# Seven block products per pair of token tiles in a second mixture layer

## The chip, the core and the metric

One core of a Trainium2 chip runs attention and two mixture layers as one kernel. Its engines are TensorE (PE), VectorE (DVE), ScalarE (ACT), GpSimd (POOL) and SyncE (SP), which issues the DMAs. The metric is the device time of one execution in microseconds; less is better.

## The reference, cut to what matters

```python
def _moe2_ref(x, w_in, w_out, g_ln):          # x: 2304 x 512, w_in: 512 x 1024, w_out: 1024 x 512
    h = x @ w_in
    h_max = np.max(h, axis=-1, keepdims=True)
    e = np.exp(h - h_max)
    sm = e / (np.sum(e, axis=-1, keepdims=True) + 1e-09)
    solu = h * sm
    mu = np.mean(solu, axis=-1, keepdims=True)
    var = np.mean((solu - mu) ** 2, axis=-1, keepdims=True)
    ln = (solu - mu) / np.sqrt(var + 1e-06) * g_ln
    return ln @ w_out
```

Ahead of it stand causal attention with a decay (32 heads, 576 positions, 64 wide) and a first mixture layer of 2304 x 512 tokens with 2048 hidden units, whose result is this layer's x. The weights come in 64-bit floats; the kernel turns each chunk into 32-bit values itself.

## The kernel before, in words

Every product is made of three: each operand is split into a high part and a low part (a rounded 32-bit format of TensorE, and what it leaves), and high x high, high x low and low x high are summed in PSUM.

The order of the work isn't written out by hand. All work is handed to a planner (`add` of class Plan) as operations with an engine, a cost in ns (`dve(n)`, `act_p(n)`, `mm(n)`), the keys that they read and write, and a priority; `run` goes through a modelled time, lets each engine take the ready operation of lowest priority value (TensorE) or lowest ready time plus priority (the others), and writes the instructions out in that order. On the chip each engine's queue is in that order, and semaphores hold an instruction until its operands are there. DMAs are all issued from SP's queue, in order.

Attention comes first, with the first mixture layer's early jobs between (256 tokens each, three of eight groups of weights). Then `extend` closes attention's memory, and wide jobs of 512 tokens (`job_wide`) finish the first layer: first the other tokens with the first three groups, then all tokens with the other five. The last job has 256 tokens. While these run, the second layer's weights are loaded (`load_w`): a raw chunk of 512 KB is converted by ScalarE and VectorE (lines 805 to 812), and split into a high and a low part (lines 392 to 403 or 824 to 826). All eight weight tiles (128 x 1024, high and low) stay in SBUF: slots w0 to w5 and two late ones.

The second layer runs over 18 tiles of 128 tokens (`tile2`). For each pair of tiles the x of 256 tokens (512 deep, 4 chunks of 128) is loaded, cast to its high part (line 392) and subtracted to its low part (line 402). A tile's first product is four groups of six products of 128x512 (line 1125) into a PSUM tile of two banks, `ph`, of which there are two. Then VectorE takes the maximum of 1024 (line 1130), ScalarE the exponential (1132), VectorE the reciprocal and h times softmax (1135) and the centring (1138), ScalarE the squares (1139), GpSimd the inverse root. TensorE transposes the centred tile in two groups of four (line 1156); ScalarE makes the high part (1159), VectorE the low part (1160); 24 products (lines 1168 to 1170) give the output, which ScalarE scales (1174) and a DMA writes.

Tile 0's first product goes to the first layer's banks (`x2`), with priorities among the last job's products. `second` opens the second layer's pools when everything ahead has ended except DMAs (key m2); `third` gives the first layer's banks to transposes and outputs when tile 0's softmax is done with them (key m3). In the planner the first products of a later tile have priority 5000 + i, its transposes 5100 + i, its outputs 5200 + i.

Of the kernel before, what the change touches and what calls it, by code (L numbers as in the profile page):

```python
# [18 lines left out]
CH = 256  # L19
# [11 lines left out]
HM = 3  # L31
# [227 lines left out]
def kernel(  # L259
# [39 lines left out]
    xc_d = dram.tile([KD, 128, NT], F32, name="xc_d")  # L299

# [487 lines left out]
    def load_w(t, srcs, key, raws, sc=None, b=BW, after=()):  # L788

        for g, src in enumerate(srcs):  # L790
            hi, lo = (lambda x=x, g=g: x[:, 512 * g:512 * g + 512] for x in t)
            rn = slot(raws, 2)
            rt = rawsets[raws][rn]
            kr = (raws, rn)
            scv = None if sc is None else sc[:, g:g + 1]
            jr = slot("wr", 2)
            r = wr[jr]
            kw = ("wr", jr)
            add("SP", 650, lambda rt=rt, src=src: nc.sync.dma_start(
                out=rt()[:, :, 0:2 if wide else 1].rearrange("p (c n) e -> p c (n e)", c=src.shape[1]),  # L800
                in_=src.bitcast(U32)), (), [kr], b, bytes=524288, after=after)
            if wide:


                add("ACT", act_s(512), lambda rt=rt, r=r: nc.scalar.activation(
                    out=f32(r), in_=f32(rt())[:, :, 1], func=AF.Abs, scale=2.0 ** -112), [kr], [kw], b)
                add("DVE", dve2(512), lambda r=r: nc.vector.tensor_scalar(
                    out=r, in0=r, scalar1=3, scalar2=None, op0=ALU.logical_shift_left), (), [kw], b, lk=True)
                add("DVE", dve(512), lambda rt=rt, r=r: nc.vector.scalar_tensor_tensor(
                    out=r, in0=rt()[:, :, 0], scalar=29, in1=r, op0=ALU.logical_shift_right, op1=ALU.bitwise_or),  # L810
                    [kr], [kw], b, lk=True)
                add("DVE", dve(512), lambda rt=rt, r=r: nc.vector.scalar_tensor_tensor(
                    out=r, in0=rt()[:, :, 1], scalar=0x80000000, in1=r, op0=ALU.bitwise_and, op1=ALU.bitwise_or),
                    [kr], [kw], b, lk=True)
                rv = lambda r=r: f32(r)
                kv = kw
            else:
                rv = lambda rt=rt: f32(rt())[:, :, 0]
                kv = kr
            if sc is None:  # L820
                copy(hi, rv, 512, [kv], [key + (g, 0)], b)
                tt(lo, rv, lambda hi=hi: f32(hi()), 512, ALU.subtract, [kv, key + (g, 0)], [key + (g, 1)], b)
            else:
                add("ACT", act_s(512), lambda rv=rv, hi=hi, scv=scv: nc.scalar.activation(
                    out=hi(), in_=rv(), func=AF.Copy, scale=scv), [kv, "gl"], [key + (g, 0)], b)
                add("DVE", dve(512), lambda rv=rv, hi=hi, lo=lo, scv=scv: nc.vector.scalar_tensor_tensor(
                    out=lo(), in0=rv(), scalar=scv, in1=f32(hi()), op0=ALU.mult, op1=ALU.subtract),
                    [kv, "gl", key + (g, 0)], [key + (g, 1)], b, lk=True)
# [8 lines left out]
    def load_fp(fp, ta, tb, ka, kb, raws, b=BW, after=()):  # L837
        c = slice(fp * 256, fp * 256 + 256)
        a = w_in[:, c].rearrange("(k p) n -> p k n", p=128)
        load_w(ta, (a[:, 0:2], a[:, 2:4]), ka, raws, None, b, after)  # L840
        a = w_out[c, :].rearrange("(k p) n -> p k n", p=128)
        load_w(tb, (a[:, 0:1], a[:, 1:2]), kb, raws, None, b, after)
        weights[fp] = (ta, tb, ka, kb)
# [245 lines left out]
    NTILE = NT // 128  # L1089

    def tile2(i, part=None):

        c, o = divmod(i, 2)
        o *= 128
        jc, jh, jd, js = c % 2, i % 2, i % 3, i % 4
        kx = [H(("xx", 2)), H(("xx", 3))] if c == 0 else [[("x2h", jc)], [("x2l", jc)]]
        x_hi = (lambda: xhis[0]) if c == 0 else (lambda: late["xh"][jc])
        x_lo = (lambda: xlos[0]) if c == 0 else (lambda: late["xl"][jc])
        if i == 0:
            h = lambda: x2ps[0].rearrange("p k n -> p (k n)")  # L1100
            kh, ke, kd, ks, ext, ext2 = ("x2", 0, 0), ("wraw", 0), ("wraw", 1), "sm0", [], []
            e, d = (lambda t=t: f32(t).rearrange("p n e -> p (n e)") for t in wraw)
            sm = lambda: sm0
        else:
            h, e, d, sm = (lambda a=a, b=b: late[a][b] for a, b in (("ph", jh), ("e2", jh), ("d2", jd), ("sm", js)))
            kh, ke, kd, ks, ext, ext2 = ("ph", jh), ("e2", jh), ("d2", jd), ("sm", js), ["m2"], ["m2"]
        if o == 0 and c:
            t, kt = (lambda: xraw, H(("xx", 0))) if c == 1 else (lambda: late["xr"][jc], [("xr", jc)])
            add("SP", 650, lambda: nc.sync.dma_start(
                out=t(), in_=x2_d[:, :, c * CH:(c + 1) * CH].rearrange("k p t -> p k t")),  # L1110
                [("x2d", c, k) for k in range(KD)] + (ext if c > 1 else []),
                kt, 0, bytes=524288)
            copy(x_hi, t, 1024, kt + ext, kx[0], B2)
            tt(x_lo, t, lambda: f32(x_hi()), 1024, ALU.subtract, kt + kx[0], kx[1], B2)
        sp = lambda a: sm()[:, a:a + 1]
        V, A = nc.vector, nc.scalar
        if part == 1:
            return tile2_out(i, jd, d, sp, kd, ks)
        for kc in range(KD):
            def h_mm(kc=kc):  # L1120
                wh, wl = w2[kc]
                a, b = x_hi()[:, kc, o:o + 128], x_lo()[:, kc, o:o + 128]
                for st_, mv in ((a, wh), (a, wl), (b, wh)):
                    for n in range(0, DFF2, 512):
                        nc.tensor.matmul(h()[:, n:n + 512], st_, mv[:, n:n + 512],  # L1125
                                         start=kc == 0 and mv is wh and st_ is a, stop=kc == KD - 1 and st_ is b)

            add("PE", 6 * mm(512), h_mm, kx[0] + kx[1] + wkeys((f"w{kc}",)) + ext, [kh] + ([("x2", 0, 1)] if i == 0 else []),
                5000 + i if i else 1000 + 100 * (len(jobs) - 1) + (4 * HM if kc < KD - 1 else 99))
        add("DVE", dve(1024), lambda: V.tensor_reduce(out=sp(0), in_=h(), axis=AX.X, op=ALU.max), [kh], [ks], B3)  # L1130
        add("DVE", 70, lambda: V.tensor_scalar_mul(out=sp(1), in0=sp(0), scalar1=-1.0), (), [ks], B3)
# [11 lines left out]
        if part is None:  # L1143
            tile2_out(i, jd, d, sp, kd, ks)
# [132 lines left out]
    for i in range(8):  # L1277
        t = wslot[i] if i < 2 * FP1 else (Lazy(), Lazy())
        if i >= 2 * FP1:
            late["w2b", i - 2 * FP1] = t  # L1280
# [12 lines left out]
    for i in range(1, NTILE):  # L1293
        tile2(i)
# [44 lines left out]
```

## Time and profile before

| | us |
|---|---|
| Median of 3 runs | 833.92 (833.08 to 834.3) |
| The profiled execution | 835.25 |
| Its span, first to last instruction | 833.5 |
| TensorE busy, of the span | 808.5 (97%) |
| VectorE / ScalarE busy | 501.0 / 505.7 |
| Share of TensorE in the chain that ended last | 80% |

The span is what the trace shows; 1.75 us of the profiled execution lie around it. A product's record ends when its pipe has drained (0.39 us for 512 columns), while the next one starts earlier, so records of one engine overlap, and the distance of starts is the price of a product.

### The profile page before, as it was taken

To read this page: it belongs to the slowest core of one execution; us is meant where nothing else is said; L and a number is where in the kernel's file an instruction comes from. 1 tells how busy PE (TensorE), PEld (TensorE's weight loads), DVE (VectorE), ACT (ScalarE), POOL (GpSimd) and SP (SyncE) were. 2 spreads that over 40 slices of the span, in tenths; PEclk is the share of its full clock that TensorE was granted. 3 is DMA by queue.
4 is the path that set the end of the run, shared out by engine and by line. 5 is a ranking of instruction groups with operands and counts; after the bars stand their busy time and mean duration, and the time that the engine had idled before them with its cause. 6 is when DMAs were issued, how large, how long until landed. Compare 5 with 4: busy or idle time off the path is not lost.

```text
span 833.5 us, 12764 instructions
## 1 busy us (share of the span) xinstructions
PE 808.5 (97%) x4687; PEld 688.0 (83%) x4687; DVE 501.0 (60%) x1030; ACT 505.7 (61%) x1021; POOL 105.6 (13%) x139
## 2 busy tenths in 40 slices
PE   8889999999899999999999999999999999999998
PEld 7577889889889988788878888788998888888886
DVE  7899988878776387888841321313828445544350
ACT  8888898788578467777744365545625343433342
POOL 3563201210210011121100000000001000000000
PEclk9999999999999999999999999999999999999999
DMA  8754744643422598573460210400621111100001
GB/s 291 219 191 166 228 130 118 210 151 93 147 99 67 168 316 288 191 244 126 149 202 1 72 55 1 149 3 1 203 71 57 39 51 35 42 26 14 25 26 51
DMA packets 60407, 98.24 MB, mean 118 GB/s; under 512 B 5656, under 2 KB 34712, under 8 KB 60344
## 3 DMA queue, kind: packets, MB, share of 16 engines
q1 hardware_dynamic: 60344, 97.43, 36.4%
q8 instruction: 37, 0.61, 0.3%
q14 instruction: 26, 0.21, 0.1%
HBM read 69.02 MB, written 28.39 MB: 117 GB/s over the span
## 4 chain that ended last, share of the span: by engine, by line
PE 80%; DVE 10%; DMA 4%; issue 3%; ACT 2%; SPq 0%; POOL 0%; DVEq 0%; ACTq 0%; POOLq 0%
PE h L1029 13%; PE ph L1125 11%; PE x L1029 8%; PE x2w L1036 6%; PE x2w L1037 6%; PE x2w L1035 6%; PE S L600 5%; PE O L760 4%; PE po L1168 4%; PE po L1170 4%; PE po L1169 4%; PE PT L674 4%; PE pt L1156 2%; DVE e L635 2%; DVE rs L617 1%
## 5 line engine op out<-in xcount | busy, mean ns | idle before, releaser
L979 DVE SCALAR_TENSOR_TENSOR gl<-r,b_sb,gh 128x512 fp32r<-128x512 f32 x71 | 54.0, 761 | 119.1 <-ACT gh L988 119.1
L659 ACT ACTIVATE e<-e,m 128x128 f32<-128x128 f32 (+4 forms) x144 | 83.8, 584 | 15.1 <-DVE m L635 14.8
L1037 PE MATMUL x2w<-gh,u 128*128 128x512 f32 (+1 forms) x200 | 73.6, 368 | 0.0
L1036 PE MATMUL x2w<-gl,u 128*128 128x512 f32 (+1 forms) x200 | 73.6, 368 | 0.0
L1035 PE MATMUL x2w<-gh,u 128*128 128x512 f32 (+1 forms) x200 | 73.6, 368 | 0.0
L635 DVE CUSTOM_DVE_ANT_0 e<-S,mask 128x384 f32<-128x384 f32 (+4 forms) x136 | 61.3, 487 | 12.6 <-PE S L600 11.3
L1125 PE MATMUL ph<-w,xh 128*128 128x512 f32 x256 | 68.8, 391 | 0.0
L674 PE MATMUL PT<-ident,e 128*128 128x128 f32 x384 | 60.0, 282 | 6.4 <-DVE pbl L682 3.5
L1160 DVE TENSOR_TENSOR dl<-pt,dh 128x512 fp32r<-128x512 f32 x36 | 24.1, 688 | 60.8 <-ACT dh L1159 60.8
L1125 PEld LDWEIGHTS ph<-w,xh 128*128 128x128 f32 x256 | 47.9, 188 | 10.2
L965 ACT ACTIVATE r<-h 128x512 f32<-128x512 f32 x46 | 27.2, 591 | 47.2 <-PE h L1029 47.1
L682 DVE TENSOR_TENSOR pbl<-PT,pbh 128x512 fp32r<-128x512 f32 (+1 forms) x80 | 49.3, 625 | 10.5 <-ACT pbh L398 10.2
L398 ACT CAST pbh<-PT 128x512 fp32r<-128x512 f32 (+2 forms) x96 | 45.5, 493 | 11.7 <-PE PT L674 10.0
L674 PEld LDWEIGHTS PT<-ident,e 128*128 128x128 f32 x384 | 42.8, 142 | 11.8 <-DVE pbl L682 3.6
L1029 PE MATMUL h<-xhl,w 128*128 128x256 f32 (+1 forms) x312 | 51.7, 299 | 0.0
L1159 ACT CAST dh<-pt 128x512 fp32r<-128x512 f32 x36 | 20.3, 586 | 49.0 <-PE pt L1156 36.6
L988 ACT ACTIVATE gh<-r,b_sb 128x512 fp32r<-128x512 f32 x65 | 46.9, 722 | 2.1 <-DVE r L969 0.6
L972 ACT ACTIVATE r<-r,s_sb 128x512 f32<-128x512 f32 x63 | 45.6, 724 | 2.1
L1029 PE MATMUL h<-xh,u 128*128 128x256 f32 (+1 forms) x216 | 46.1, 330 | 0.0
L760 PE MATMUL O<-pbh,vs 128*128 128x320 f32 (+2 forms) x160 | 43.0, 289 | 0.5 <-ACT xt L398 0.4
L1036 PEld LDWEIGHTS x2w<-gl,u 128*128 128x128 f32 x200 | 37.7, 189 | 6.3
L1037 PEld LDWEIGHTS x2w<-gh,u 128*128 128x128 f32 x200 | 37.7, 188 | 6.2
(229 smaller groups left out, 2116.3 us busy)
## 6 DMA issues: line engine op xcount, KB each, us to landing
raw<-in_qk_dram SPq DMA_DIRECT2D x12, 608.0 KB
wraw<-in_moe_w_in_dram SPq DMA_DIRECT2D x14, 512.0 KB
wraw<-in_moe_w_out_dram SPq DMA_DIRECT2D x14, 512.0 KB
xs_d<-xt SPq DMA_DIRECT2D x16, 320.0 KB
raw<-in_moe_w_in_dram SPq DMA_DIRECT2D x10, 512.0 KB
raw<-in_moe_w_out_dram SPq DMA_DIRECT2D x10, 512.0 KB
xp<-x2p_d SPq DMA_DIRECT2D x18, 256.0 KB
x_d<-xo SPq DMA_DIRECT2D x18, 256.0 KB
```

The lines of the kernel that those rows point to most:

```text
L635: nc.vector.tensor_tensor_reduce(out=e_, in0=sp, in1=mk, scale=-scale, scalar=init, op0=ALU.add, op1=ALU.min, accum_out=acc)
L659: nc.scalar.activation(out=e[:, c], in_=e[:, c], func=AF.Exp, scale=-1.0, bias=m[:, j:j + 1], accum_out=rt[:, cols[j]:cols[j] + 1])
L674: nc.tensor.transpose(pt[:, kb, :], e[:, 128 * kb:128 * kb + 128], ident)
L682: add("DVE", dve(n), lambda: nc.vector.tensor_tensor(out=lo, in0=src, in1=f32(hi), op=ALU.subtract), [kp, kh], [kl], ba)
L760: nc.tensor.matmul(pc[:, o:o + n], v_[:, kb, x, :], t[:, x, src:src + n], start=first, stop=fin, skip_group_check=True)
L979: nc.vector.scalar_tensor_tensor(out=gl, in0=r, scalar=b_sb, in1=f32(gh), op0=ALU.add, op1=ALU.subtract)
L988: add({"ACT": (act_s(512), lambda: nc.scalar.activation(out=gh, in_=r, func=AF.Identity, bias=b_sb)), "DVE": (dve2(512), lambda: nc.vector ...
L1029: nc.tensor.matmul(t, w_, v_[:, kc, :], start=kc == 0 and first and x == 0, stop=kc == KD - 1 and x == 2, skip_group_check=True)
L1035: nc.tensor.matmul(t, a_, gh, start=start, stop=False, skip_group_check=True)
L1036: nc.tensor.matmul(t, a_, gl, start=False, stop=False, skip_group_check=True)
L1037: nc.tensor.matmul(t, b_, gh, start=False, stop=stop, skip_group_check=True)
L1125: nc.tensor.matmul(h()[:, n:n + 512], st_, mv[:, n:n + 512], start=kc == 0 and mv is wh and st_ is a, stop=kc == KD - 1 and st_ is b)
```

## The change

A pair of tiles (256 tokens) times the 512 x 1024 weights is taken as a product of 2 x 2 blocks by 2 x 2 blocks: a block of x is 128 tokens by 256 of depth, a block of weights 256 by 512. Instead of the eight block products, seven are made, of sums and differences of blocks on both sides (a scheme of Winograd's).

On the side of the weights the sums are made once: `stage_w2` converts the same raw chunks, makes the differences (`minus`), splits seven blocks and the four tiles of output weights into high and low parts, in slots w2 and w3, and writes all eleven to DRAM (`w2_d`); `fetch` reads them back into slots: eight before the second layer, three of the output weights after its pools are open. On the side of x, `prep2` makes four sums of 256 per pair and splits seven operands. `pair2` gives the products: seven groups of six, on two banks in turn; after each, ScalarE or VectorE takes the bank: one copy, two sums of bank and tile (`plus`) and four last sums (`final`), which write the negated h to SBUF with a running minimum in place of the maximum. The softmax then reads h from SBUF instead of PSUM, in tiles of which there are six; its order and the outputs are as before. Pair 0 takes the place of tile 0: five groups with a priority within the last job, two behind it. A scratch size for DMA descriptors is set to 1024 where the program is made.

```diff
+    NB2 = 7 + DFF2 // 256
+    w2_d = dram.tile([NB2, 2, 128, 1024], F32, name="w2_d")
...
+    def value(src, t, kt, raws, b=BW, after=()):
...
+    def split(hi, lo, khi, klo, rv, kv, b, scv=None):
...
+    def stage_half(b, q, rv, kv, scv=None):
+        k = slot("stg", 4)
+        i, h = 2 + k // 2, k % 2
+        hi, lo = (lambda x=x: x[:, 512 * h:512 * h + 512] for x in wslot[i])
+        ks = [(f"w{i}", h, x) for x in range(2)]
+        split(hi, lo, ks[0], ks[1], rv, kv, 0, scv)
+        for x, t in enumerate((hi, lo)):
+            add("SP", 650, lambda x=x, t=t: nc.sync.dma_start(out=w2_d[b, x, :, 512 * q:512 * q + 512], in_=f32(t())), [ks[x]],
+                [("w2d", b, q, x)], 0, bytes=262144)
+    def stage_w2():
...
+        for q in range(2):
+            chunk(0, 0, 1, q)
+            chunk(3, 0, 0, q)
+            minus(1, 0, 3)
+            put(3, 0, q)
+            put(1, 3, q)
...
+        for i in range(DFF2 // 128):
...
+            stage_half(7 + i // 2, i % 2, lambda r=r: f32(r), kw, gl_sb[:, i:i + 1])
+    def fetch(b, t, key, r=()):
+        for x in range(2):
+            add("SP", 650, lambda x=x: nc.sync.dma_start(out=f32(t[x][:, :]), in_=w2_d[b, x]), [("w2d", b, q, x) for q in range(2)] + list(r),
+                [key + (q, x) for q in range(2)], 0, bytes=524288)
+    def prep2(g):
+        j = g % 2
+        b_ = B2 - 3000 * (g == 1)
...
+        for o, x, y, op in ((0, lambda: a(1, 0), lambda: a(1, 1), ALU.add), (1, lambda: sv(0), lambda: a(0, 0), ALU.subtract),
+                            (2, lambda: a(0, 0), lambda: a(1, 0), ALU.subtract), (3, lambda: a(0, 1), lambda: sv(1), ALU.subtract)):
+            tt(lambda o=o: sv(o), x, y, 256, op, kr + ext, ks, b_)
...
+        for s_, src, n, k in ((slice(0, 2), lambda: raw_[:, :, 128:256], 512, kr), (slice(2, 3), lambda: a(1, 1), 256, kr),
+                              (slice(3, 7), lambda: st().rearrange("p k n -> p (k n)").rearrange("p (k n) -> p k n", n=128), 1024, ks)):
...
+            copy(lambda s_=s_: part(oh, s_), src, n, k + ext + ["ext"], [kh], b_)
+            tt(lambda s_=s_: part(ol, s_), src, lambda s_=s_: f32(part(oh, s_)), n, ALU.subtract, k + [kh] + ext, [kl], b_)
+    def pair2(g):
...
+        def final(t, f, y, u):
...
+                V.tensor_tensor_reduce(
+                    out=hr()[:, 512 * f:512 * f + 512], in0=bank_(), in1=uv, scale=-1.0, scalar=sm()[:, 0:1] if a else 3.0e38, op0=ALU.add,
+                    op1=ALU.min, accum_out=sm()[:, a:a + 1])
...
+        def plus(o, y, u):
+            (bank_, kb), (uv, ku), (ov, ko) = banks[y], tmp[u], tmp[o]
+            add("DVE", dve(512), lambda: V.tensor_tensor(out=ov, in0=bank_(), in1=uv, op=ALU.add), [kb, ku], [ko], B3 - 2000)
+        steps = [(0, 0, 0, lambda: add("ACT", act_p(512), lambda: A.copy(out=tmp[0][0], in_=banks[0][0]()), [banks[0][1]], [tmp[0][1]],
+                                       B3 - 2000)),
+                 (4, 4, 1, lambda: plus(1, 1, 0)), (1, 1, 0, lambda: final(0, 0, 0, 0)), (5, 5, 1, lambda: plus(2, 1, 1)),
+                 (3, 3, 0, lambda: final(1, 1, 0, 2)), (2, 6, 1, lambda: final(1, 0, 1, 1)), (6, 2, 0, lambda: final(0, 1, 0, 1))]
+        for x, (a, b, y, then) in enumerate(steps):
+            def mms(a=a, b=b, y=y, x=x):
...
+                for kc in range(2):
+                    c = slice(512 * kc, 512 * kc + 512)
+                    for z, (s_, mv) in enumerate(((oh, wh), (oh, wl), (ol, wh))):
+                        nc.tensor.matmul(o, s_[:, a, kc, :], mv[:, c], start=x < 5 and kc == 0 and z == 0, stop=kc == 1 and z == 2,
+                                         skip_group_check=True)
...
+            add("PE", 6 * mm(512), mms, [("oh", j, s_), ("ol", j, s_)] + wkeys(w2[b][1]) + ext + ["ext"], [banks[y][1]],
+                5000 + 2 * g if g else 1000 + 100 * (len(jobs) - 1) + (4 * HM if x < 5 else 99))
+            then()
-        for kc in range(KD):
-            def h_mm(kc=kc):
...
-        add("DVE", dve(1024), lambda: V.tensor_reduce(out=sp(0), in_=h(), axis=AX.X, op=ALU.max), [kh], [ks], B3)
-        add("DVE", 70, lambda: V.tensor_scalar_mul(out=sp(1), in0=sp(0), scalar1=-1.0), (), [ks], B3)
-        add("ACT", 1090, lambda: A.activation(out=e(), in_=h(), func=AF.Exp, bias=sp(1), accum_out=sp(2)), [kh], [ke, ks], B3)
+        add("ACT", 1090, lambda: A.activation(out=e(), in_=d(), func=AF.Exp, scale=-1.0, bias=sp(1), accum_out=sp(2)), [kd, "m2"], [ke, ks], B3)
...
+    prep2(0)
...
+    stage_w2()
...
+    for b, i in ((0, 0), (4, 1), (1, 2), (5, 3)):
+        fetch(b, wslot[i], (f"w{i}",))
+    fetch(3, late["w2b", 1], ("w7",))
+    fetch(6, late["w2b", 0], ("w6",))
+    for b, i in ((2, 4), (7, 5)):
+        fetch(b, wslot[i], (f"w{i}",))
     n1 = len(P.ops)
-    tile2(0, 0)
+    first_ = pair2(0)
     add("NONE", 0, second, (), ["m2"], after=[op["n"] for op in P.ops[:n1] if not op["bytes"]])
-    add("NONE", 0, third, ["m2"], [("x2", 0, 0), "m3"])
-    tile2(0, 1)
-    for i in range(1, NTILE):
-        tile2(i)
+    add("NONE", 0, third, ["m2"], [("x2", 0, 0), ("x2", 0, 1), "m3"])
+    for b, t in enumerate(homes):
+        fetch(8 + b, t, (f"v{b}",), ["m2"])
+    prep2(1)
+    tail2(first_)
+    for g in range(1, NPR):
+        if g > 1:
+            prep2(g)
+        tail2(pair2(g))
```

## Rows read from the trace of the kernel before

**Rows 1.** Page, busy shares and 40 slices; PEclk is the granted clock in tenths.
```profile
PE 808.5 (97%) x4687; PEld 688.0 (83%) x4687; DVE 501.0 (60%) x1030; ACT 505.7 (61%) x1021; POOL 105.6 (13%) x139
...
PE   8889999999899999999999999999999999999998
...
PEclk9999999999999999999999999999999999999999
DMA  8754744643422598573460210400621111100001
```

**Rows 2.** Windows of two steady periods: length, busy us (instructions) by engine, clock, DMA.
```profile
675.10:698.89 23.79, 23.79 (x113) 19.70 (x113) 11.28 (x22) 9.06 (x17) 1.48 (x4) 1.00 0.14 45
698.89:722.72 23.83, 23.83 (x113) 19.70 (x113) 11.40 (x22) 9.06 (x17) 1.48 (x4) 1.00 0.14 45
```

**Rows 3.** Chain of waits in time order, second layer: start, us, what, count.
```profile
675.10 10.89 PE ph L1125 x48
...
698.89 10.93 PE ph L1125 x48
```

**Rows 4.** VectorE groups by line and shape: names, shapes, count, busy us, mean ns.
```profile
L1160 DVE TENSOR_TENSOR dl<-pt,dh 128x512 fp32r<-128x512 f32 x36 | 24.1, 688 | 60.8 <-ACT dh L1159 60.8
...
L1135 DVE SCALAR_TENSOR_TENSOR e<-ph,sm,e 128x1024 f32<-128x1024 f32 x17 | 21.8, 1284 | 0.6
...
L635 DVE CUSTOM_DVE_ANT_0 e<-S,mask 128x512 f32<-128x512 f32 x32 | 21.0, 678 | 3.4 <-PE S L600 3.4
L1130 DVE TENSOR_REDUCE sm<-ph 128x1 f32<-128x1024 f32 x17 | 20.7, 1218 | 0.1
...
L635 DVE DVE_READ_ACCUMULATOR2_ANT m<- 128x1 f32 x160 | 13.0, 82 | 0.0
...
L1078 DVE TENSOR_TENSOR xo<-x2w,xp 128x512 f32<-128x512 f32 x18 | 12.1, 688 | 21.2 <-DMA xp<-x2p_d 14.7 <-PE x2w L1037 6.5
...
L402 DVE TENSOR_TENSOR xl<-xr,xh 128x1024 fp32r<-128x1024 f32 x7 | 8.6, 1223 | 5.6 <-ACT xh L392 5.6
...
L682 DVE TENSOR_TENSOR pal<-PT,pah 128x256 fp32r<-128x256 f32 x14 | 5.9, 419 | 5.8 <-ACT pah L398 5.7
```

**Rows 5.** Timeline at the join of the layers: start us, us, engine, line.
```profile
618.52 1.41 DVE L1078 TENSOR_TENSOR xo<-x2w,xp 128x512 f32<-128x512 f32 x2 [4.30 <-PE x2w L1037]
...
619.04 1.55 PE L1125 MATMUL x<-w,xhl 128*128 128x512 f32 x6
...
619.96 1.05 ACT L392 CAST xh<-xraw 128x1024 fp32r<-128x1024 f32 x1 [6.53 <-DVE xo L1078]
...
620.42 5.60 PE L1125 MATMUL ph<-w,xhl 128*128 128x512 f32 x24
...
625.87 1.07 PE L1125 MATMUL ph<-w,xh 128*128 128x512 f32 x4
```

**Rows 6.** Chain of waits, tile 0 among the last job.
```profile
600.70 4.11 PE x L1125 x18
```

**Rows 7.** Windows of attention and of the last jobs.
```profile
100.00:250.00 150.00, 145.63 (x1199) 131.10 (x1197) 122.28 (x317) 118.94 (x310) 21.76 (x22) 0.99 0.44 136
400.00:500.00 100.00, 99.31 (x439) 81.91 (x438) 37.47 (x57) 54.00 (x83) 4.94 (x6) 1.00 0.30 94
500.00:600.00 100.00, 99.31 (x493) 84.29 (x492) 35.44 (x54) 54.35 (x82) 1.40 (x2) 1.00 0.23 74
```

**Rows 8.** Windows around 215 us, in attention.
```profile
210.00:215.00 5.00, 3.22 (x27) 2.76 (x27) 4.97 (x9) 2.68 (x6) 1.60 (x1) 1.00 0.27 79
215.00:220.00 5.00, 4.34 (x23) 3.74 (x23) 2.97 (x6) 2.27 (x7) 0.00 (x0) 0.66 0.91 289
```

**Rows 9.** TensorE timeline there: start us, us, line, [idle before <-releaser].
```profile
215.66 0.55 PE L760 MATMUL O<-pah,vs 128*128 128x256 f32 x1 [2.44 <-DVE rs L617]
```

**Rows 10.** Timeline of SyncE's queue: weight loads beside the wide jobs.
```profile
388.32 17.51 SPq L799 DMA_DIRECT2D wraw<-in_moe_w_in_dram  x6
```

**Rows 11.** TensorE timeline, the last product.
```profile
829.16 0.39 PE L1170 MATMUL po<-v,dl 128*128 128x512 f32 x1
```

More of the change, by code (lines that the diff above doesn't have):

```diff
@@ L790, in load_w @@
+    def load_w(t, srcs, key, raws, b=BW, after=()):
         for g, src in enumerate(srcs):
             hi, lo = (lambda x=x, g=g: x[:, 512 * g:512 * g + 512] for x in t)
[L792 to L795, printed above, removed]
             jr = slot("wr", 2)
[L797 to L828, printed above, removed]
+            r, kw = wr[jr], ("wr", jr)
@@ L830, in wkeys @@
+            value(src, lambda r=r: r, kw, raws, b, after)
+            split(hi, lo, key + (g, 0), key + (g, 1), lambda r=r: f32(r), kw, b)
     def wkeys(key):
@@ L1089 @@
     NTILE = NT // 128
[L1091 to L1103, printed above, removed]
-        else:
[L1105 to L1114, printed above, removed]
-        sp = lambda a: sm()[:, a:a + 1]
-        V, A = nc.vector, nc.scalar
-        if part == 1:
-            return tile2_out(i, jd, d, sp, kd, ks)
-        for kc in range(KD):
-            def h_mm(kc=kc):
[L1121 to L1129, printed above, removed]
-        add("DVE", dve(1024), lambda: V.tensor_reduce(out=sp(0), in_=h(), axis=AX.X, op=ALU.max), [kh], [ks], B3)
-        add("DVE", 70, lambda: V.tensor_scalar_mul(out=sp(1), in0=sp(0), scalar1=-1.0), (), [ks], B3)
-        add("ACT", 1090, lambda: A.activation(out=e(), in_=h(), func=AF.Exp, bias=sp(1), accum_out=sp(2)), [kh], [ke, ks], B3)
-        add("DVE", 70, lambda: V.tensor_scalar_add(out=sp(2), in0=sp(2), scalar1=1e-9), (), [ks], B3)
@@ new lines @@
+    NPR = NT // 256
+    def stage_half(b, q, rv, kv, scv=None):
[7 more added lines that the diff above has]
+                [("w2d", b, q, x)], 0, bytes=262144)
@@ new lines, in stage_w2, with chunk, minus, put @@
+    def stage_w2():
+        flat = lambda i: late["raw"][i // 2].rearrange("p n e -> p (n e)")[:, 512 * (i % 2):512 * (i % 2) + 512]
+        tw = [lambda i=i: flat(i) for i in range(4)]
+        kt = [("tw", i) for i in range(4)]
+        take([("wraw2", 0), ("wraw2", 1)] + kt)
+        def chunk(i, k, f, q):
+            o = 256 * k + 128 * q
+            value(w2_in[o:o + 128, 512 * f:512 * f + 512].rearrange("(k p) n -> p k n", p=128), tw[i], kt[i], "wraw", 0, [ext])
+        def minus(o, x, y):
+            tt(lambda: f32(tw[o]()), lambda: f32(tw[x]()), lambda: f32(tw[y]()), 512, ALU.subtract,
+               [kt[i] for i in (x, y) if i != o], [kt[o]], 0)
+        def put(i, b, q):
+            stage_half(b, q, lambda: f32(tw[i]()), kt[i])
+        for q in range(2):
[4 more added lines that the diff above has]
+            put(1, 3, q)
+            chunk(2, 1, 1, q)
+            minus(1, 2, 1)
+            minus(0, 2, 0)
+            put(2, 2, q)
+            put(1, 4, q)
+            put(0, 5, q)
+            chunk(3, 1, 0, q)
+            minus(1, 3, 1)
+            put(3, 1, q)
+            put(1, 6, q)
+        for i in range(DFF2 // 128):
+            jr = slot("wr", 2)
+            r, kw = wr[jr], ("wr", jr)
+            value(w2_out[128 * i:128 * i + 128, :].rearrange("(k p) n -> p k n", p=128), lambda r=r: r, kw, "wraw", 0, [ext])
+            stage_half(7 + i // 2, i % 2, lambda r=r: f32(r), kw, gl_sb[:, i:i + 1])
+        take(kt + [("wraw2", 0), ("wraw2", 1)])
@@ L1235, in extend @@
         late_tiles(late["w2b", 1])
+        ops = ctx.enter_context(tc.tile_pool(name="ops", bufs=1))
+        late["oh"], late["ol"] = ([ops.tile([128, 7, 2, 128], F32R, name=n)] for n in ("oh0", "ol0"))
+        late["sm1"] = ops.tile([128, 128], F32, name="sm1")
         p2 = late["p2"] = ctx.enter_context(ExitStack())
```

132 lines of the change are left out of this document (102 added, 30 removed).

## Prediction

> **What bounds the kernel now.** I read the page's shares and slices first: TensorE is busy for 97% of the span, from slice 8 on nearly without a break, at a granted clock of 0.9 or more, while VectorE's share of the span is 60% and the DMA engines' is a few tenths after slice 20 [rows 1]. A busy TensorE alone proves little, so I next took the windows of two periods of the second mixture layer: 23.79 and 23.83 us, TensorE busy in all of each, VectorE for 11.3 and 11.4 us, clock 1.00 [rows 2]. The chain of waits, in order of time, says what fills such a period: 48 products of line 1125 in a row (one pair of token tiles) take 10.89 and 10.93 us [rows 3], or 0.2273 us each; the rest is 16 transposes and 48 output products. So this stage is bound by the number of TensorE's instructions. It waits for nobody there, and what is taken from it comes off the end, until something else is late.
>
> **What is removed.** Before: 4 chunks x 6 products x 18 tiles = 432 products 128x512 of line 1125. After: 7 blocks x 6 = 42 for each of 9 pairs = 378. 54 x 0.2273 = **12.27 us** less. Operands, width and weight loads per product are of the same kind, so I keep the price. Transposes and output products stay as many.
>
> One rule of the Trainium skill would make the gain smaller (TensorE: Matmul & The Clock Gate, Back-to-back issue gap): it puts sustained 512-column products about 131 ns apart. By it 54 products would be worth 7.1 us; the rows show 227 ns, and the measurement decides, so this gets no chance of its own.
>
> **What is added on VectorE and ScalarE, per pair.** VectorE loses two maxima of 1024 (1.218 us each) and one 1024-wide low part (1.223), 3.66 us. It gains [rows 4]: four last sums with a running minimum, like line 635's 128x512 row (0.678 + 0.082), 3.04 us; two sums bank + tile, like line 1078's (0.688), 1.38; four operand sums of 256, like line 682's (0.419), 1.68; low parts of 512, 256 and 1024 (0.69 as in line 1160, 0.42, 1.22), 2.33. From the 11.4 us of a period [rows 2] that makes 11.4 - 3.66 + 8.43 = 16.2 us, of a period that would be 23.83 - 6 x 0.2273 = 22.47: **72%, against 48% before**. ScalarE gains a bank copy and 768 columns of casts, some 1.4 us on 9.06, and stays near half. Neither becomes the bound by its sum. But seven groups of six products (1.36 us each) now alternate between two banks, and a bank must be emptied while the other one fills: about 0.2 us of pipe and semaphore, 0.76 of VectorE and 0.1 back make 1.06 us (an estimate from [rows 4, 5]). That leaves 0.3 us of slack, less than what one 1.28 us instruction in VectorE's way takes.
>
> The order of TensorE's queue is fixed ahead by the planner, which puts output products of an earlier pair where it foresees a late bank; it counts VectorE's instructions at about a tenth less than the rows (69 + 1.04 x 512 = 601 ns for the 688 of line 1160), so some waits are unforeseen. The trace of before has no such coupling in this stage and no wait (lower bound 0). Upper bound: the attention part has it, with VectorE busy 122.28 of 150 us (82%), and there TensorE idles 150 - 145.63 = 4.37 us, 2.9% [rows 7]. On eight steady pairs (180 us) that is 5.2 us. 72% is nearer to the attention row, but the output products are a better cover than attention has; I take **2.5 us**.
>
> **The join of the layers.** Now the last job's last product ends at about 619.2, six products of tile 0 follow, VectorE empties the banks until 619.9, and the pools change hands; tile 1 runs from 620.42 with operands that were there before, and under its 5.5 us the next operands are cast and subtracted, so line 1125 goes on at 625.87 without a gap [rows 5]. After: pair 0's first five groups go in among the last job (as 18 products of tile 0 do now [rows 6]), and only two groups, 2.73 us, stand behind the last job. The pool change comes 0.75 us after its end. From there pair 1 needs four operand sums (1.68), a low part of 512 (0.69) and semaphores (0.2): its first group starts 3.3 us after the job, against 2.73 of cover, a gap of 0.6 us. Its second group needs the 1024-wide cast and low part (1.05 + 1.22) with pair 0's last sums in between: 0.9 us more. The next bank sum can stand behind a 1.28 us instruction of pair 0's softmax: 0.8. No outputs are ready to fill these. That is 2.3 us; I take **2.5**, between 0 (the planner brings pair 0 in later) and 6: as much again for the softmax of tiles 0 and 1 in the way, and a fall of the clock. The trace shows one behind a wait of 2.44 us that ends at 215.66 [rows 9]: 0.66 in those 5 us [rows 8], which is 3.4 us of them at the lower level, 1.2 GHz, and so 1.7 us lost.
>
> **Weights through DRAM.** The conversion is the same 16 chunks. Added are 8 subtractions and 6 more splits of 512 (14 times 0.69 on VectorE, and 6 casts), 44 writes of 256 KB and 22 reads of 512 KB (23 MB; at the 289 GB/s of one row [rows 8], 80 us of transfers). They lie between 400 and 600 us, where VectorE is busy 37.5 and 35.4 of 100 us and DMA 0.30 and 0.23 [rows 7]; the nearest work, six such loads with their splits from 388.32 on [rows 10], ran beside a TensorE busy 99% of the time. On SyncE's in-order queue a write waits for its split, with the last jobs' loads of x and partial sums behind it; these are needed some us later. Bounds 0 and 2; I take **0.5**. Three output blocks (3.1 MB, 11 us at that rate) are fetched only after the pool change; the first is needed behind pair 1's 9.5 us and tile 0's softmax, so I cost them at nothing; uncovered they cost up to 4 us. The end stays: about 4 us from the last product (829.16) to the span's end [rows 11]. The earlier parts keep their instructions.
>
> **Sum.** -12.27 + 2.5 + 2.5 + 0.5 = **-6.8 us**. The profiled execution took 835.25 us (span 833.5), 1.33 above the median, so its span would fall to 826.7; from the median, 833.92 - 6.8 = **827.1 us**. Its own range, with each of the three losses half of its way to either bound: 824.4 to 831.0.
>
> **Rivals.**
> - Clean: every wait is foreseen and filled, and the join costs 1 us or less. 833.92 - 12.3 + 0.5 to 2.5 = 822 to 824.5. For it: no wait in 675 to 794 us now, with transposes and low parts that also hang on VectorE. Against: banks are now refilled within 1.4 us.
> - Late blocks or a bad join: the fetched output blocks, or the first pairs' VectorE work (four operand sums, softmax and sums together ask for some 19 us in the first 13), hold TensorE 4 to 6.5 us more: 831 to 833.6. Against: 11 us of transfer behind some 12 of products.
> - The bank exchange binds (slower): each of the 63 groups waits for its bank because VectorE, in order, is in the middle of softmax. The gain is gone at 12.27 / 63 = 0.195 us a group, less the join and staging at 0.15. A wait of 0.3 us, the mean rest of a busy VectorE, unfilled, costs 19 us: 833.92 - 12.3 + 19 + 3 = 843.6. Against: output groups of 0.68 us as fill.
> - The clock falls within the stage: TensorE's short waits between groups bring it to the lower level, as the wait of 2.44 us did [rows 8, 9], at 1.7 us a fall. One fall per pair is 15 us: about 842; three falls, 832. Against: in 100 to 250 us the clock is 0.99 with many short waits [rows 7]. The Trainium skill has this mechanism (TensorE: Matmul & The Clock Gate, A second HAM failure mode: psum-queue depth-cycling): cycling through PSUM banks leaves small idles between groups, and the clock oscillates. No row here shows it for short waits.
>
> **How the numbers follow.** Chances: forecast 0.52, clean 0.20, late blocks 0.10, bank exchange 0.10, clock 0.08. About 0.2% (1.7 us) is what a measurement tells from no change. Faster: 0.52 + 0.20 + 0.06 + 0.04 = 0.82; same: 0.07; slower: 0.11. The range 822 to 834 takes in the first three and part of the clock's.
>
> **What would show it.** Right: line 1125's successor has 378 products at 0.227 us; a period of 22.5 to 22.9 us in steady pairs with VectorE at 70 to 74%; waits for TensorE of 2 to 4 us between about 620 and 635; none new in 400 to 600. Wrong: waits of TensorE on the bank sums of over 0.2 us a group; a clock under 0.95 in windows after 620; waits on DMA of w2_d; x loads landing late before 600. If the transposes and outputs fill every bank wait, my 2.5 us for the steady pairs falls away.

## The result and the profile after

The changed kernel takes 841.58 us (median of 4 runs, 839.99 to 845.39), the one before 833.5 in the same comparison: a ratio of 1.0103 (95% interval 1.0066 to 1.014). It is slower by 8 us, where 6.8 us of gain were forecast. The profiled execution is the longest of the four, 845.39 us with a span of 843.6, so its losses add up to some 4 us more than the median shows.

The page of after: 54 products fewer, as the change says, and yet a longer span; TensorE's share of it has gone from 97 to 95% [rows 1].

```profile
span 843.6 us, 12980 instructions
...
PE 804.1 (95%) x4633; PEld 678.2 (80%) x4633; DVE 533.7 (63%) x1112; ACT 520.1 (62%) x1054; POOL 150.2 (18%) x178
...
PE   8889999999899999999999999999998899999998
PEclk9899999999999999999999999999999999999999
```

Where TensorE waits, I read from a table of waits by the instruction that waited. For 600 to 850 us the trace of before has no wait of TensorE at all; after has these (us in total, times, longest):

```profile
PE ph L1231 <- DVE sm L1209: 5.3, 9, 0.8
PE ph L1231 <- ACT r L1219: 2.3, 1, 2.3
PE ph L1231 <- DVE wr L1217: 1.3, 2, 0.9
PE ph L1231 <- DVE r L1217: 1.2, 2, 0.8
PE x L1231 <- DVE sm L1209: 0.8, 1, 0.8
PE x L1231 <- DVE wr L1217: 0.7, 1, 0.7
PE ph L1231 <- ACT wr L1219: 0.7, 1, 0.7
```

L1231 is the new first product, L1209 a last sum (`final`), L1217 a sum of bank and tile (`plus`), L1219 ScalarE's copy of a bank. With two small ones the waits make 12.8 us over 63 groups, 0.20 us a group; those on VectorE's sums (L1209, L1217) alone are 9.3 us, 0.15 a group. To weigh stretches I also took, from the trace, by how much the distances of successive products' starts exceed the usual ones of their kinds (so a lower clock counts too):

| stretch, us | before | after |
|---|---|---|
| 300 to 600 (wide jobs, staging) | 3.7 | 9.2 |
| 600 to 660 (join) | 0.1 | 10.8 |
| 660 to 850 (steady pairs) | 0.5 | 10.3 |

That is some 26 us of new loss against 12.3 removed, and the span is 10.1 us longer. Of the 3.6 us between, 1.8 are attention, which ended earlier in this execution; the rest I couldn't place.

**Steady pairs.** The answer to [rows 2], windows from a repeated wait to its next occurrence (length, busy us by engine, clock, DMA):

```profile
717.68:741.42 23.74, 22.86 (x107) 18.42 (x106) 14.48 (x31) 10.77 (x18) 4.67 (x8) 1.00 0.06 23
741.42:765.14 23.72, 22.85 (x107) 18.41 (x106) 13.67 (x28) 9.80 (x16) 3.97 (x7) 1.00 0.06 23
```

A period lasts as long as before, with six products fewer in it: TensorE is now idle for 0.9 us of each at full clock, and VectorE is at 58 to 61%. So no engine is full. The timeline of VectorE and of TensorE at the start of the first window shows what is waited for (start us, us, engine, line, [idle before <-releaser]):

```profile
716.99 0.69 DVE L1209 CUSTOM_DVE_ANT_0 hr<-ph,xraw 128x512 f32<-128x512 f32 x1 [1.47 <-PE ph L1231]
717.61 0.08 DVE L1209 DVE_READ_ACCUMULATOR2_ANT sm<- 128x1 f32 x1
717.72 0.75 DVE L1209 CUSTOM_DVE_ANT_0 hr<-ph,wr,sm 128x512 f32<-128x512 f32 x1
...
717.68 0.40 PE L1287 MATMUL po<-v,dl 128*128 128x512 f32 x1
718.54 0.73 PE L1231 MATMUL ph<-w,oh 128*128 128x512 f32 x2 [0.46 <-DVE sm L1209]
```

The group that starts at 718.54 writes bank 0. Bank 0 had been read by 717.68 (716.99 + 0.69). The group starts 0.07 us after the *other* bank's last sum has ended (717.72 + 0.75 = 718.47). Both banks are halves of one PSUM tile `ph`, and the planner keeps a key for each half. It foresaw a wait for the half, while the program waits for the tile; run 2 below tests this reading.

**The join.** After 300 us, two stretches of 10 us, one at the staging and one at the join, have a granted clock of 0.83, all others up to 830 us 1.00; with two levels, 1.2 and 2.4 GHz, that is 3.4 us at the lower one and 1.7 us lost in each:

```profile
420.00:430.00 10.00, 7.58 (x24) 5.57 (x24) 10.00 (x11) 3.03 (x7) 6.58 (x4) 0.83 1.01 382
630.00:640.00 10.00, 6.99 (x23) 5.01 (x22) 6.53 (x17) 5.01 (x9) 8.08 (x7) 0.83 1.01 368
```

At the join TensorE waits 2.34 us for the second pair's bank copy (L1219). The copy stands behind two exponentials of pair 0's softmax in ScalarE's queue, and next to it GpSimd spends 4.17 us on low parts of operands, which I had put on VectorE:

```profile
629.58 4.17 POOL L405 TENSOR_TENSOR ol<-xhl,oh 128x512 fp32r<-128x512 f32 x4 [99.84 <-ACT oh L394]
...
631.65 1.15 ACT L1251 ACTIVATE e<-wraw,sm 128x1024 f32<-128x1024 f32 x1 [1.01 <-DVE sm L1209]
...
632.80 1.13 ACT L1251 ACTIVATE e<-wraw,sm 128x1024 f32<-128x1024 f32 x1
...
633.93 0.56 ACT L1219 COPY r<-ph 128x512 f32<-128x512 f32 x1
...
634.54 1.22 PE L1231 MATMUL ph<-w,oh 128*128 128x512 f32 x2 [2.34 <-ACT r L1219]
```

### The profile page after: what moved, and what is told of

Same layout as the page of the kernel before. It is cut to its first block, busy times and chain, and to the rows that moved or that the text cites. A ratio compares the mean times of both kernels' runs of the same rounds, so it can differ in the third digit from the quotient of the medians.

```text
span 843.6 us, 12980 instructions
## 1 busy us (share of the span) xinstructions
PE 804.1 (95%) x4633; PEld 678.2 (80%) x4633; DVE 533.7 (63%) x1112; ACT 520.1 (62%) x1054; POOL 150.2 (18%) x178
## 4 chain that ended last, share of the span: by engine, by line
PE 63%; DVE 16%; DMA 9%; ACT 6%; issue 4%; SPq 1%; POOL 0%; DVEq 0%; ACTq 0%; POOLq 0%
PE ph L1231 9%; PE h L1033 9%; PE x L1033 5%; PE S L602 5%; PE x2w L1040 4%; PE O L762 4%; PE x2w L1041 4%; PE x2w L1039 4%; PE po L1287 4%; PE po L1285 4%; PE po L1286 4%; PE PT L676 3%; DMA raw<-in_moe_w_in_dram 2%; DMA raw<-in_moe_w_out_dram 2%; DMA wraw<-in_moe_w_in_dram 2%
## 5 line engine op out<-in xcount | busy, mean ns | idle before, releaser
L969 ACT ACTIVATE r<-h 128x512 f32<-128x512 f32 x46 | 27.2, 592 | 56.0 <-PE h L1033 55.7
L1231 PE MATMUL ph<-w,oh 128*128 128x512 f32 x160 | 52.2, 408 | 9.4 <-DVE sm L1209 3.8
L684 DVE TENSOR_TENSOR pbl<-PT,pbh 128x512 fp32r<-128x512 f32 (+1 forms) x80 | 49.2, 624 | 10.3 <-ACT pbh L400 10.0
L676 PEld LDWEIGHTS PT<-ident,e 128*128 128x128 f32 x384 | 43.1, 143 | 10.2 <-DVE pbl L684 3.6
L992 ACT ACTIVATE gh<-r,b_sb 128x512 fp32r<-128x512 f32 x66 | 47.6, 721 | 2.9 <-PE x2w L1041 1.6
L1231 PEld LDWEIGHTS ph<-w,oh 128*128 128x128 f32 x160 | 29.7, 193 | 20.6 <-DVE sm L1209 6.9
L1285 PE MATMUL po<-v,dh 128*128 128x512 f32 x108 | 44.1, 408 | 0.0
```

The source lines that it names most:

```text
L676: nc.tensor.transpose(pt[:, kb, :], e[:, 128 * kb:128 * kb + 128], ident)
L684: add("DVE", dve(n), lambda: nc.vector.tensor_tensor(out=lo, in0=src, in1=f32(hi), op=ALU.subtract), [kp, kh], [kl], ba)
L1231: nc.tensor.matmul(o, s_[:, a, kc, :], mv[:, c], start=x < 5 and kc == 0 and z == 0, stop=kc == 1 and z == 2, skip_group_check=True)
L1285: nc.tensor.matmul(ot, dh[:, j, :], wh[:, c], start=j == 0, stop=False)
```

## The experiments

Times stand as ratios to the kernel before on the same chip (832.3 to 832.5 us in the three batches of runs, 833.5 beside the changed kernel), with a 95% interval; 0.001 is 0.83 us. Differences in us between runs are taken from the ratios.

**1. What 54 products are worth.** The kernel before; its first product leaves out the last quarter of depth for odd tiles.

```diff
-        for kc in range(KD):
+        for kc in range(KD - i % 2):
```

> The kernel before, with the last quarter of the depth left out of the first product of every second tile of the second layer (54 products of 128x512 fewer, nothing added). If a product is worth its distance of starts (0.2273 us), 12.3 us less than before: 821.2 against 833.5. By the Trainium skill's 131 ns a product (TensorE: Matmul & The Clock Gate, Back-to-back issue gap) it would be 7.1 us less: 826.4.

Measured: 818.84 us, 0.9849 (0.982 to 0.9877), 12.6 us less (10.2 to 15.0 by the interval), or 0.233 us a product. The 12.3 us of the forecast lie inside, the 7.1 us at 131 ns a product do not. The removal was priced right; all of the miss is in what is added.

**2. A PSUM tile for each bank.** The changed kernel with `ph` as four tiles of one bank; VectorE, ScalarE and GpSimd execute the same instructions in the same order.

```diff
-            banks = [(lambda i=i: late["ph"][j][:, 512 * i:512 * i + 512], ("ph", j, i)) for i in range(2)]
+            banks = [(lambda i=i: late["ph"][2 * j + i], ("ph", j, i)) for i in range(2)]
-        late["ph"] = tiles(..., [128, DFF2], F32, "ph", 2)
+        late["ph"] = tiles(..., [128, 512], F32, "ph", 4)
```

> The changed kernel with one PSUM tile for each bank of ph in place of one tile for two banks; instructions and planner's order otherwise alike. Theory A, waits are held for whole tiles, so that a group of products waits for the emptying of the other bank too and a bank sum for the other bank's products: the 0.6 us waits of steady pairs (6 us from 700 to 830 us, 3 from 660 to 700) mostly go, 833 to 836 us. Theory B, VectorE is late by itself (the planner counts it too short, or it is too full): no change, 840 to 843 us.

Measured: 829.78 us, 0.997 (0.9954 to 0.9986): 11 us less than the changed kernel, and now faster than before. All nine waits on `sm L1209` of `ph` are gone, and after 660 us TensorE waits for nothing. At the place of the timeline above, the group on bank 0 now starts 0.24 us after that bank's sum has ended (710.83 + 0.69 = 711.52) and while the other bank's is still running (to 712.32):

```profile
710.83 0.69 DVE L1209 CUSTOM_DVE_ANT_0 hr<-ph,xraw 128x512 f32<-128x512 f32 x1 [1.47 <-PE ph L1231]
...
711.57 0.75 DVE L1209 CUSTOM_DVE_ANT_0 hr<-ph,wr,sm 128x512 f32<-128x512 f32 x1
...
711.76 0.62 PE L1231 MATMUL ph<-w,oh 128*128 128x512 f32 x2
```

TensorE's chain of waits, in order of time, has first products every 22.6 us (709.43 to 732.03), the period that the prediction worked out:

```profile
709.43 1.36 PE ph L1231 x6
...
732.03 1.37 PE ph L1231 x6
```

Of TensorE's waits after 600 us only those of pair 0 and of the join are left:

```profile
PE ph L1231 <- ACT r L1219: 2.3, 1, 2.3
PE x L1231 <- DVE sm L1209: 0.8, 1, 0.8
PE x L1231 <- DVE wr L1217: 0.7, 1, 0.7
PE ph L1231 <- ACT wr L1219: 0.7, 1, 0.7
```

**3. The same from the planner's side.** The changed kernel, with the shared tile, but 600 ns more counted for each sum out of a bank.

```diff
-            add("DVE", 8 + dve(512), fin, ...
+            add("DVE", 600 + dve(512), fin, ...
-            add("DVE", dve(512), lambda: V.tensor_tensor(out=ov, in0=bank_(), in1=uv, op=ALU.add), ...
+            add("DVE", 600 + dve(512), lambda: V.tensor_tensor(out=ov, in0=bank_(), in1=uv, op=ALU.add), ...
```

> The changed kernel (841.58) with its two-bank tiles as they are, but the planner counts each bank sum on VectorE 600 ns longer, about the wait over both banks; no instruction differs. Theory A with enough outputs to fill: the planner puts outputs in front of the late groups, the waits after 660 us fall from 10 to some 3 us, 834 to 837 us. Theory A without fill, or theory B: waits only move, 840 to 843 us.

Measured: 828.8 us, 0.995 (0.9924 to 0.9976). That is 13 us less than the changed kernel, more than either theory had forecast. Of the waits of the steady pairs (after 660 us) 0.2 us are left:

```profile
PE ph L1231 <- DVE sm L1209: 0.2, 1, 0.2
```

The order of TensorE's queue has changed, and some work has gone from VectorE to other engines (8 of 1112 instructions). There are thus enough output products to stand in; the planner only had to know that the bank comes later. The shared tile costs what it costs because nothing ahead counts it.

**4. GpSimd's part.** The staging's and the operands' subtractions and casts are kept off GpSimd, in the changed kernel (e3) and on top of run 2 (e4).

```diff
+    def tt_(out, a, b, n, op, r, w, pri=0):
+        add({"DVE": (dve(n), lambda: nc.vector.tensor_tensor(out=out(), in0=a(), in1=b(), op=op), True)}, 0, 0, r, w, pri)
...
-            tt(lambda o=o: sv(o), x, y, 256, op, kr + ext, ks, b_)
+            tt_(lambda o=o: sv(o), x, y, 256, op, kr + ext, ks, b_)
```

> The changed kernel with GpSimd kept out of the weights' staging and of the preparation of x: its subtractions go to VectorE, its casts to ScalarE or VectorE. Theory C, GpSimd's subtractions hold VectorE up (its 512-wide instructions take 1.75 us beside them at 418 to 425 us, 0.69 otherwise), and this made the stalls at 419 to 426 us and at the join, with a fall of the clock behind each: 4 us back before 600 and 3 to 5 at the join, 833 to 835 us, and no window under 0.95. Theory B, VectorE is too full: its added work makes the steady pairs longer, 841 to 845 us.

> The changed kernel with both edits, one tile per bank and no GpSimd in staging and preparation. If A and C hold and are separate, their gains add: 825 to 829 us, below the kernel before. If one waits behind the other, not better than the better one alone. Theory B: 840 us or more.

Measured: e3 843.39 us, 1.0133 (1.0104 to 1.0162), so alone it gains nothing that can be told. Its time lies where theory B put it, but on the separate tiles of e4 the same work on VectorE costs nothing. e4 827.73 us, 0.9941 (0.992 to 0.9962), 2.4 us under run 2, though the two intervals touch. The traces put it at the join: the wait on the bank copy falls from 2.3 to 1.3 us, and the one on `ACT wr` (0.7) goes.

```profile
PE ph L1238 <- ACT r L1226: 1.3, 1, 1.3
```

(L1238, L1226, L1216 and L408 in these kernels are L1231, L1219, L1209 and L394 of after.) The theory that GpSimd's slow subtractions are the main loss falls; they are a share of the join. The staging's stall stays in both, at 2.5 us in e3 and 2.2 in e4.

**5. The staging's rank.** On top of e4, the staging's conversions and splits get the last place among ready work (20000 added to their ready time).

```diff
-        split(hi, lo, ks[0], ks[1], rv, kv, 0, scv, copy_, tt_)
+        split(hi, lo, ks[0], ks[1], rv, kv, LOW, scv, copy_, tt_)
```

> The kernel of the run with one tile per bank and no GpSimd in staging and preparation (827.73), with the staging's conversions, differences and splits ranked behind all other work in the planner. If the 2.9 us of stall at 419 to 423 us are the staging's instructions in the way of the job's gate on ScalarE and VectorE: 2 to 3 us less, 825 to 826, and no new wait from 400 to 450 us. If the transfers (DMA engines full from 400 to 450 us) hold the next job's x: no change, or later weights and a wait at the join.

Measured: 828.88 us, 0.9946 (0.9926 to 0.9966), no change; the stall is still there (2.1 and 0.2 us at 419 to 422 us). But the edit moved nothing: by the traces VectorE, ScalarE, GpSimd and SyncE execute the same kinds of instructions in the same order as in e4. At the stall the conversion still stands ahead of the ReLU (L979 here):

```profile
415.76 0.67 ACT L809 ACTIVATE raw<-wraw 128x512 f32<-128x512 f32 x1 [1.70 <-DMA wraw<-in_moe_w_in_dram]
...
417.89 0.58 ACT L979 ACTIVATE r<-h 128x512 f32<-128x512 f32 x1
```

A rank decides only between operations that are ready together; that the conversion was alone in the plan fits this, but isn't shown. So the run repeats e4, and says nothing on whether the staging's work or its place is the cause.

**6. Pair 0.** On top of e4: the first layer's bank pair `x2` as two tiles (e6), and in addition all seven groups of pair 0 behind the last job's products (e7).

```diff
-    x2ps = [psm.tile([128, KD, CH], F32, name="x2")]
+    x2ps = tiles(psm, [128, 2, CH], F32, "x2", 2)
...
-                5000 + 2 * g if g else 1000 + 100 * (len(jobs) - 1) + (4 * HM if x < 5 else 99))
+                5000 + 2 * g if g else 1000 + 100 * (len(jobs) - 1) + 99)
```

> The same kernel (827.73) with the first layer's two-bank tile x2 made of two one-bank tiles, so that pair 0 too has a tile for each bank. Theory A: its two waits at 607 and 611 us (0.85 and 0.95, 2.1 with what follows) go: 825.5 to 826. If these waits are the job's own (gate, VectorE): no change.

> As the run with x2 split, and all seven groups of pair 0 ranked behind the last job, 9.5 us of cover for the pool change and pair 1's operands in place of 2.7. The prediction's account of the join (cover too short): the wait at 631 us (1.45 us) goes and the time is 1 to 2 us under that run. Rival: the last job has waits of its own that pair 0 filled, and loses as much or more there: no change or 1 to 3 us slower than that run.

Measured: e6 826.99 us, 0.9918 (0.9885 to 0.9951); e7 825.63 us, 0.9915 (0.9885 to 0.9945). The two waits of pair 0 (`x L1231`, 1.5 us) go with the split, as the shared tile asks; the intervals overlap e4's, so the times alone don't show it. Moving pair 0 trades the join's wait of 1.3 us for one of 2.1 us near 655 us, on VectorE's sums behind the softmax: nothing gained that can be told.

**7. The stall of the staging.** In after's timeline of ScalarE at 415 us, a conversion of a staged weight (L801) waits 1.60 us for its load, two casts of x follow, and only then, at 416.57, the ReLU (L969) of a first product whose last instruction ended at 412.88; the gate that needs it (L992) comes at 419.38, and TensorE waits from 419.7 on:

```profile
414.97 0.67 ACT L801 ACTIVATE raw<-wraw 128x512 f32<-128x512 f32 x1 [1.60 <-DMA wraw<-in_moe_w_in_dram]
415.54 1.13 ACT L394 CAST xh<-xraw 128x512 fp32r<-128x512 f32 x2
416.57 0.59 ACT L969 ACTIVATE r<-h 128x512 f32<-128x512 f32 x1
...
419.38 0.72 ACT L992 ACTIVATE gh<-r,b_sb 128x512 fp32r<-128x512 f32 x1
```

The planner may have put the conversion first since it took the load to be there. To test this, e10 (on e7) and e11 (on the changed kernel) count a longer time for the 16 loads, and change nothing else:

```diff
-            value(w2_in[...], tw[i], kt[i], "wraw", 0, [ext])
+            value(w2_in[...], tw[i], kt[i], "wraw", 0, [ext], 150)      # bytes a ns, 340 before
```

> This is the kernel of e7_pair0_behind; only the time that the planner counts for each of the 16 loads of raw weights for the blocks in DRAM is longer (150 bytes a ns in place of 340). Loads, conversions and writes are the same ones; only their places in the queues move. In e7's trace ScalarE's ReLU of one first product of a job of the first layer stands behind a conversion of a staged weight that waited 1.66 us for its load, and behind casts of x; it ran 5 us after its product had ended, and TensorE waited 3.0 us. Theory F (the planner puts the conversion ahead of the ReLU since it takes the load to land sooner than it does): the wait at 413 to 420 us goes, 400 to 450 us lose under 1.5 us to stalls where e7 lost 5.2, and the time falls by 3 to 5 us from e7, to 821 to 823 us. Theory G (the transfers themselves, at 0.95 to 1.0 of the DMA engines' time in 390 to 450 us, or the added work on VectorE and ScalarE, make it late): a wait of 2 to 4 us stays in the same stretch and the time stays at 825 to 827 us.

> The changed kernel, with the longer count for the 16 loads and nothing else. Theory F: it loses the 4 us of its 400 to 450 us (5.1 us of stalls there) and keeps the waits on the shared tile: 836 to 839 us. Theory G: 840 to 843 us, with the stall in its place.

Measured: e10 820.96 us, 0.9853 (0.9828 to 0.9878), 5 us under e7; e11 838.55 us, 1.0073 (1.0049 to 1.0098), 2.5 us under the changed kernel. The intervals of e10 and e7 lie apart; those of e11 and the changed kernel overlap, so there the trace has to speak. In e10 TensorE has no wait at all from 395 to 450 us, at the same DMA share (0.94 in 400 to 450 us in both):

```profile
410.00:420.00 10.00, 10.00 (x46) 8.29 (x45) 9.86 (x13) 4.08 (x7) 3.16 (x3) 1.00 0.79 238
420.00:430.00 10.00, 10.00 (x45) 8.28 (x45) 7.55 (x13) 9.77 (x17) 0.00 (x0) 1.00 0.99 356
```

In e11 the waits after 600 us are those of after, line for line, and of those of 395 to 450 us only a ReLU's 0.7 us is left, which the kernel before has too:

```profile
PE x L1033 <- ACT r L969: 0.7, 1, 0.7
```

In both, the ReLU that came 3.7 us after its product in after follows it within 0.1 us (at 410.07 behind 410.03 in e11), and GpSimd still works beside it in e11. So the stall was the order of the queues, as ScalarE's shows it, and not the transfers or the amount of work.

**8. All together.** e10 with the longer count of run 3.

> e10_load_counted_slower with the longer count of e8_counted_longer for the additions out of a bank as well (600 ns each), on tiles of one bank: the closest to a version without repeated waits. If the count only stood in for the tiles, it is worth nothing on top of them (821 to 823 us, as e10); if it also mends the wait of 2.2 us near 655 us, where VectorE's additions stood behind the softmax, it is 2 us faster (819 to 821).

Measured: 820.1 us, 0.9842 (0.9816 to 0.9867). Against e10 the difference is inside the intervals. The wait of 2.1 us, near 652 us in e10, is gone; one of 0.9 us at the join is left of all waits after 600 us:

```profile
PE ph L1238 <- DVE sm L1216: 0.9, 1, 0.9
```

By its median this is the fastest version: 1.6% under the kernel before, level with the 1.5% that run 1 showed for 54 products fewer and no cost at all. It is level in part because the jobs ahead have lost a wait that before and run 1 have, the ReLU's 0.7 us at 421 to 426 us.

## Why the prediction was wrong

Point by point, with what each term measured:

| term | predicted | bounds | measured |
|---|---|---|---|
| 54 products removed | -12.27 | | -12.6 (run 1) |
| steady pairs | +2.5 | 0 to 5.2 | +9.8 in the profiled execution |
| join | +2.5 | 0 to 6 | +10.7 in the profiled execution, pair 0's waits in it |
| weights through DRAM | +0.5 | 0 to 2 | +5.5 in the profiled execution; 2.5 by e11, 5 by e10 |

**The steady pairs: the step that failed.** I took it that a bank must be emptied "while the other one fills", with 0.3 us of slack for each bank. That needs a wait for the bank. The code quoted in the change says `ph` [j] with a slice for each bank, so the tile is shared and a group also waits for the sum on the other bank; the slack is then negative for any two sums that come late together. I drew the upper bound from attention's idle share [rows 7], a stage whose own PSUM tiles hold one bank each (only two spare banks are halves of one tile), so it couldn't hold the 9.8 us. Runs 2 and 3 show the cause from both sides, 11 and 13 us, some of it at the join. The Trainium skill (Perfetto Trace Analysis, Matmuls) says that groups should rotate through PSUM banks so that one bank's evacuation overlaps the next one's products. After rotates, and where a sum on the other bank is late, the next group waits for it too (0.42 to 0.85 us after 700 us): the overlap comes here only once each bank is a tile of its own, as run 2 against after shows.

The rival "the bank exchange binds" had the place right. Its point of decision, 0.195 us a group, or 0.15 with the forecast join and staging, lies beside what was measured: 0.20 with the join's waits, 0.15 on VectorE's sums. A wait costs more than its length, though: by the distances of starts, join and steady pairs lost 20.5 us, 0.33 a group, of which 1.7 us are the clock (idle time is counted from the end of a record, which lies 0.39 us behind its start, while the next product could have started after 0.23). Its reason (VectorE in the middle of softmax) is not the one that the timeline shows for the steady pairs, where VectorE was at a sum of the other bank, and its time, 843.6 at 0.3 us a group, was too long by 2; that it came so near is partly luck, as it held 0.3 us for the mean rest of a busy VectorE, and VectorE was busy for 58 to 61%. I gave it 0.10. The argument against it, output products as fill, fails where the planner doesn't know that they are needed, as run 3 shows.

**The join.** The mechanism was named ("the softmax of tiles 0 and 1 in the way, and a fall of the clock") and lay within the bound of 6: the wait of 2.34 us behind two exponentials and 1.7 us of clock are 4 us of it. What was missing is the rest: waits on the shared `ph` tile (some 3 us: after loses 10.8 us in 600 to 660 and run 2, at full clock there, 6.3), pair 0's waits on the shared `x2` tile (1.5 us), and GpSimd on operand subtractions that I had all put on VectorE (some 2 us by e4 against run 2; 1 us of it is out of the 2.34, since the wait behind the exponentials falls to 1.3).

**Weights through DRAM.** I compared sums of busy time and transfers with the room beside them. Over 100 us the room was there: DMA share 0.79 and VectorE at 64 us in 400 to 500, against 0.30 and 37 before [rows 7]. In 400 to 450 us the DMA engines were full (0.96), but e10 runs without a stall at 0.94. What I left out was the queue that a moved conversion stands in. I named what waits behind a write on SyncE's queue, not what waits behind a conversion on ScalarE's: a ReLU, and behind it the gate and TensorE. The six loads of [rows 10], on which I rested, ran with the DMA engines less full.

**Clock.** In the steady pairs, where two waits of 0.4 to 0.9 us recur in each period, it stays at 1.00, so that rival is out there. After 300 us it fell in two other places, at 1.7 us each.

**Late blocks.** TensorE has no wait on a DMA after 600 us, so the fetched blocks were in time. The bad join, which that rival also named, came, but with 10.7 us where it had some 6.5 to 9.

**By the steps that the prediction named.** 378 products: yes. A period of 22.5 to 22.9 us: 23.7 in after, 22.6 in run 2. VectorE at 70 to 74%: 58 to 61%, with GpSimd busy for 4 to 4.7 us of a period against 1.5 before. A wait of 2 to 4 us at 620 to 635: yes, 2.34. No new waits in 400 to 600: wrong, 2.1 us at 420. Of the signs of being wrong, the clock under 0.95 after 620 came (0.83), the waits on `w2_d` didn't, and the waits on the bank sums stayed below their mark of 0.2 us a group (0.15): the mark was too high, since a wait costs more than its length.

**What stays open.** Why the lower rank of run 5 moved nothing, and so what a real change of the staging's place by rank would do. How much of the join is whose: its parts were measured on top of one another, and attention, which runs 1 to 3 leave alone, ends anywhere from 271 to 277 us in the profiled executions, so single spans don't settle a us or two. How the median's 8 us divide: the profiled execution is 3.8 us above it, with a mean clock of 0.991 where the other three have 0.998 to 1.0, so the two falls of the clock may well be its own. And a plan moves as a whole: a count changed for 16 loads moves other instructions too, so in e10's profiled execution the wait near 651 us comes with a fall of the clock (0.83 in 650 to 660) that e7's doesn't have.

## What to carry to other kernels

Before alternating buffers are priced by slack, look at what object the wait is held for: two banks in one PSUM tile are one buffer to the program, even where the plan has a key for each. Of an instruction that is moved into a busy stretch, ask for each engine's in-order queue what stands behind it if its input is late by 2 us; the sums of busy time don't show this. An order that is planned ahead is as good as its counts: one corrected count (a sum out of a bank) brought back what separate tiles did, another (a load) took the stall of the staging away. And see in the trace that an edit moved what it was to move before its time is read: run 5's didn't.

## What the runs showed of the hardware that was not expected

A 512-wide VectorE instruction with two SBUF operands, 0.69 to 0.75 us alone, takes 1.75 us where GpSimd's subtractions follow one another beside it; the two engines alternate, one start every 1.7 us each (in after's timeline at 418 us):

```profile
418.70 1.77 DVE L404 TENSOR_TENSOR raw<-raw,raw 128x512 f32<-128x512 f32 x1
420.40 1.75 DVE L983 SCALAR_TENSOR_TENSOR gl<-r,b_sb,gh 128x512 fp32r<-128x512 f32 x1
...
418.19 1.74 POOL L405 TENSOR_TENSOR raw<-raw,raw 128x512 f32<-128x512 f32 x1
419.89 1.71 POOL L405 TENSOR_TENSOR w<-raw,w 128x512 fp32r<-128x512 f32 x1
```

The Trainium skill (SBUF — State Buffer, SBUF: two separate sides) has this as an exclusive lock of a shared port, in which the loser blocks for a whole instruction; the alternation agrees. TensorE's second wait at 420 us (0.56 on the gate, then 1.49 on its low part, the 1.75 us instruction above) is partly this; but without GpSimd in the staging (e3, e4) the stall is as long, 2.5 and 2.2 us, nearly all of it on the gate.

The clock doesn't follow from the length of a wait. In after it fell behind waits of 2.3 us (join) and of 0.6 and 1.5 us within 2 us (staging); in run 2 the same two places have the same waits (2.3; 0.5 and 1.4 us) at a clock of 1.00:

```profile
630.00:640.00 10.00, 6.99 (x30) 5.13 (x29) 7.65 (x19) 6.14 (x11) 7.24 (x6) 1.00 0.98 354
...
420.00:430.00 10.00, 8.07 (x34) 5.93 (x32) 9.83 (x9) 4.22 (x8) 7.41 (x5) 1.00 0.97 364
```

A wait of 2.1 us had a fall behind it in e10 (second line) and none in e7 (first):

```profile
650.00:660.00 10.00, 7.92 (x43) 6.29 (x42) 9.99 (x23) 6.08 (x13) 2.98 (x4) 1.00 0.10 34
...
650.00:660.00 10.00, 7.66 (x31) 5.63 (x31) 8.40 (x18) 4.86 (x10) 1.87 (x4) 0.83 0.17 52
```

The prediction priced a fall by one such place [rows 8, 9]; in these traces a wait of over 2 us has one behind it in some cases and not in others.
